# Where the 480-column tiles begin in SBUF: a fused attention and SwiGLU kernel

## The chip, the cores and the metric

The kernel runs on one core of one Trainium2 chip. The metric is the device time of one execution in microseconds; lower is better. Three runs of the kernel before gave 1454.55, 1455.09 and 1456.19 us, a median of 1455.09 us.

## The reference

Two stages, on 4 batches of 12416 rows of 128 float32 numbers. The first is an attention through 32 inducing rows, the second a SwiGLU with 1536 hidden columns:

```python
def mab(q, kv):
    s = scale * (q @ kv.transpose(0, 2, 1))
    s = s - s.max(-1, keepdims=True)
    a = np.exp(s)
    a /= a.sum(-1, keepdims=True) + 1e-09
    return a @ kv
h = mab(I, x)                 # 32 rows attend to the 12416 rows of a batch
x = mab(x, h)                 # each row attends to those 32 rows
...
g = x @ w_gate
silu = g * (1.0 / (1.0 + np.exp(-g)))
val = x @ w_val
return silu * val @ w_out
```

Some shortened; all of it is float32. The 49664 rows of the second stage are the output's rows.

## The kernel before, in words

Rows of a batch are handled as columns: a tile holds up to 512 rows of x side by side, and TensorE streams them past weights that are loaded first. A batch is cut into 25 column tiles (COLS): one of 512 columns, then four each for the six entries of FC that follow the first. FC = [4, 16, 16, 16, 15, 15, 15] counts blocks of 32, so that tiles 0 to 12 of a batch have 512 columns and tiles 13 to 24 have 480. Each tile goes through 12 steps t, one for each 128 of the 1536 hidden columns (NT).

The second attention is folded into the weights: for each batch its 32 averages are multiplied into w_gate and w_val, which gives tw (L392, two buffers of 3072 columns). What is left of x in a tile is a *stack*: 128 partitions with the attention's weights split into a high and a low part (a_hi, a_lo), copied together by four DMAs of SP's queue (spread, L490; L499). A stack lies in one of three slots.

For each tile and t there is a unit of work:
- front (L680): two matmuls, L691 and L692, with tw as the loaded weights and the stack as the stream. They give g and v in PSUM (tile gv).
- gate (L695): ACT takes silu of g (L697). value (L699): DVE multiplies by v (L705); the product h stays in PSUM for three of the twelve t.
- split (L707): ACT, in some units DVE, rounds h to h_hi (L713), and POOL, or DVE for three of the twelve t, takes the rest as h_lo (L715).
- back (L719): three matmuls into one PSUM bank o: h_hi past wo_lo (L729), h_hi past wo_hi (L730), h_lo past wo_hi (L731). After t = 11 DVE copies the bank out and SP stores it (L738, L740).

PE's order is fixed by the loop at L769: the front of one unit, then the back of a unit that is about five units older, then the next front. So L691, L692, L729, L730, L731 repeat, and before each matmul its weights are loaded (the PEld rows of a profile). Around a change of width the front is of one width and the back of the other for some five units. The next batch's attention is laid between the units by slots (plan, L561), nearly all of it in 512-column stretches of the batches before the last; batch 0 has its own start, written out as lists of tokens.

The stack, h_hi and h_lo are tiles of WB = WF + 64 = 576 columns (2304 bytes a partition), of which a tile of work uses up to 512. Where it begins in them is set by AT, in float32 elements, for the stack, h_hi and h_lo:

```python
AT = (16, 48, 48), (0, 0, 0)                                            # L37
return AT[u > NG * FC.count(max(FC))]                                   # L200, at(u): second triple from tile 13 on
st.stack[u] = stp.tile([P, WB], F32R, name="stack")[:, at(u)[0]:][:, :WF]   # L487
u.hi = hip.tile([P, WB], F32R, name="h_hi")[:, u.at[1]:u.at[1] + WF]        # L711
u.lo = lop.tile([P, WB], F32R, name="h_lo")[:, u.at[2]:u.at[2] + WF]        # L712
```

In the program's memory map, modulo 256 bytes in a partition, tw, wo_hi and wo_lo begin at 224, every slot of the stack at 160, every slot of h_hi and h_lo at 32. A piece of weights is 128 columns, 512 bytes, so every piece of them has the same remainder.

Of the kernel before, what the change touches and what calls it, by code (L numbers as in the profile page):

```python
# [33 lines left out]
W = 32 * max(CH)  # L34
WF = 32 * max(FC)
WB = WF + 64
AT = (16, 48, 48), (0, 0, 0)  # L37
NT = DFF // P
SCALE = 1.0 / math.sqrt(C)

# [65 lines left out]
def induced_set_attention_then_swiglu(ctx: ExitStack, tc: tile.TileContext, xt, xn, ind, wgv, wo, out):  # L106
# [91 lines left out]
    def at(u):  # L198

        return AT[u > NG * FC.count(max(FC))]  # L200

# [637 lines left out]
```

## Time and profile before

| | |
|---|---|
| median of three runs | 1455.09 us |
| span of the profiled execution | 1453.1 us |
| TensorE: share busy, granted clock | 99%, 1.000 |
| chain that ended last: share of TensorE | 95% |
| busy shares of ACT, POOL, DVE | 88%, 83%, 82% |
| front matmuls L691 over 512 / 480 columns | 624 / 576 |
| back matmuls L729 over 512 / 480 columns | 612 / 576 |

The span is the time from the first instruction to the last of the execution that was profiled; that execution has no separate time beside it, so the median of the runs stands for it, 2.0 us above the span. The chain of work is followed back from the last instruction to whatever released each step. Matmuls overlap each other, so that the length of one in the profile is longer than the distance between the starts of two.

### The profile page before, as it was taken

The numbers are of one execution on the slowest core, as the hardware profiler recorded it, in microseconds if no ns is written. First come the engines' busy times: TensorE is split into PE (matmuls) and PEld (weight loads), VectorE is DVE, ScalarE is ACT, GpSimd is POOL, SyncE is SP. The second block draws the span as 40 slices with busy tenths as digits, with TensorE's granted clock in tenths as the row PEclk, the third lists the DMA queues.
The fourth block names the chain that finished last, engine by engine and source line by source line (L and its number), as shares of the span: only waits on it lengthen the run. The fifth ranks groups of instructions, "written<-read, shape, count | busy, mean of one in ns | idle before, by whom it ended". The sixth has DMA issues, their size and how long they took to land.

```text
span 1453.1 us, 24926 instructions
## 1 busy us (share of the span) xinstructions
PE 1441.8 (99%) x7452; PEld 1173.5 (81%) x7452; DVE 1187.8 (82%) x2080; ACT 1281.9 (88%) x2388; POOL 1207.9 (83%) x995
## 2 busy tenths in 40 slices
PE   8999999999999999999999999999999999999999
PEld 5577788788887787888888778688888888888887
DVE  6888778887888788888788778988888878878877
ACT  5888898799998887999999888799999999999997
POOL 1689778888998778898899878879889889889987
PEclk9999999999999999999999999999999999999999
DMA  9233522321143242211123522321111111111110
GB/s 369 68 98 126 185 74 97 106 64 56 36 138 136 88 137 106 70 52 42 35 69 111 189 78 93 107 79 35 42 36 42 37 44 37 40 40 38 39 41 21
DMA packets 50822, 119.80 MB, mean 82 GB/s; under 512 B 11392, under 2 KB 28288, under 8 KB 50688
## 3 DMA queue, kind: packets, MB, share of 16 engines
q1 hardware_dynamic: 50688, 118.22, 24.9%
q8 instruction: 59, 0.97, 0.3%
q14 instruction: 75, 0.61, 0.1%
HBM read 62.87 MB, written 25.43 MB: 61 GB/s over the span
## 4 chain that ended last, share of the span: by engine, by line
PE 95%; DMA 2%; ACT 1%; POOL 1%; DVE 0%; SPq 0%; issue 0%; DVEq 0%; ACTq 0%; POOLq 0%
PE gv L691 18%; PE o L729 18%; PE gv L692 18%; PE o L730 18%; PE o L731 18%; PE gv L270 2%; PE o L318 1%; DMA s_all<-wgv 1%; DMA xt<-xt 1%; PE o L270 1%; PE o L727 1%; POOL h_lo L715 0%; ACT silu L697 0%; PE gv L420 0%; ACT h_hi L713 0%; PE gv L398 0%
## 5 line engine op out<-in xcount | busy, mean ns | idle before, releaser
L715 POOL TENSOR_TENSOR h_lo<-h,h_hi 128x512 fp32r<-128x512 f32 (+1 forms) x890 | 1110.9, 1273 | 198.4 <-ACT h_hi L713 140.4
L697 ACT ACTIVATE silu<-gv 128x512 f32<-128x512 f32 (+1 forms) x1200 | 704.7, 588 | 109.3 <-PE gv L691 76.3
L705 DVE TENSOR_TENSOR h<-gv,silu 128x512 f32<-128x512 f32 (+1 forms) x891 | 594.5, 668 | 199.0 <-ACT silu L697 147.7
L713 ACT CAST h_hi<-h 128x512 fp32r<-128x512 f32 (+1 forms) x788 | 474.7, 602 | 30.1 <-DVE h L705 25.3
L691 PE MATMUL gv<-stack,tw 128*128 128x512 f32 (+1 forms) x1200 | 465.9, 388 | 2.1 <-DVE stack L543 1.3
L692 PE MATMUL gv<-stack,tw 128*128 128x512 f32 (+1 forms) x1200 | 461.5, 385 | 0.7 <-ACT silu L697 0.4
L729 PE MATMUL o<-h_hi,wo_lo 128*128 128x512 f32 (+1 forms) x1188 | 458.4, 386 | 0.0
L730 PE MATMUL o<-h_hi,wo_hi 128*128 128x512 f32 (+1 forms) x1188 | 456.9, 385 | 0.0
L731 PE MATMUL o<-h_lo,wo_hi 128*128 128x512 f32 (+1 forms) x1188 | 456.3, 384 | 0.0
L691 PEld LDWEIGHTS gv<-stack,tw 128*128 128x128 f32 x1200 | 225.4, 188 | 50.5 <-ACT tw L412 2.6
L729 PEld LDWEIGHTS o<-h_hi,wo_lo 128*128 128x128 f32 x1188 | 223.0, 188 | 51.8 <-issue 12.1
L692 PEld LDWEIGHTS gv<-stack,tw 128*128 128x128 f32 x1200 | 224.9, 187 | 47.8 <-ACT silu L697 4.2
L731 PEld LDWEIGHTS o<-h_lo,wo_hi 128*128 128x128 f32 x1188 | 222.6, 187 | 40.5 <-POOL h_lo L715 0.4
L730 PEld LDWEIGHTS o<-h_hi,wo_hi 128*128 128x128 f32 x1188 | 223.1, 188 | 38.9
L705 DVE TENSOR_TENSOR gv<-gv,silu 128x512 f32<-128x512 f32 (+1 forms) x297 | 201.8, 680 | 40.2 <-ACT silu L697 39.1
L715 DVE TENSOR_TENSOR h_lo<-gv,h_hi 128x512 fp32r<-128x512 f32 (+1 forms) x297 | 197.3, 664 | 0.9
L713 ACT CAST h_hi<-gv 128x512 fp32r<-128x512 f32 (+1 forms) x294 | 167.5, 570 | 4.9 <-DVE gv L705 3.9
L738 DVE COPY ob<-o 128x512 f32<-128x512 f32 (+1 forms) x100 | 66.3, 663 | 0.8 <-PE o L731 0.8
L713 DVE CAST h_hi<-h 128x512 fp32r<-128x512 f32 (+1 forms) x103 | 52.0, 506 | 0.0
L483 POOL TENSOR_TENSOR a_lo<-aT,a_hi 128x480 fp32r<-128x480 f32 (+2 forms) x26 | 34.6, 1330 | 0.0
L190 POOL TENSOR_TENSOR wgv_sb<-s_all 128x512 int32<-128x512 int32 x2 | 2.9, 1455 | 28.9 <-ACT s_all L178 28.9
L467 POOL TENSOR_TENSOR s_all<-s_all,sm 128x512 f32<-128x512 f32 (+2 forms) x27 | 26.1, 967 | 0.0
(155 smaller groups left out, 476.2 us busy)
## 6 DMA issues: line engine op xcount, KB each, us to landing
xt_sb<-xt SPq DMA_DIRECT2D x32, 896.0 KB, 5.2
xn_sb<-xn SPq DMA_DIRECT2D x18, 896.0 KB, 5.6
out<-ob SPq DMA_DIRECT2D x52, 256.0 KB, 2.0
out<-ob SPq DMA_DIRECT2D x48, 240.0 KB, 2.0
stack<-a_hi SPq DMA_DIRECT2D x96, 64.0 KB, 2.0
stack<-a_lo SPq DMA_DIRECT2D x96, 64.0 KB, 2.0
stack<-a_hi SPq DMA_DIRECT2D x96, 60.0 KB, 2.0
stack<-a_lo SPq DMA_DIRECT2D x96, 60.0 KB, 2.0
```

The costliest lines, as they stand in the source:

```text
L270: nc.tensor.matmul(out=ps[32 * j:32 * j + 32, 32 * (lo - b0):32 * (hi - b0)], lhsT=lhsT, rhs=st.xt[q][:, lo - CH0[q]:hi - CH0[q], j, :], s ...
L483: eng.tensor_sub(out=st.al[q][:, :n], in0=st.at[q][:, :n], in1=st.ah[q][:, :n].bitcast(F32))
L691: nc.tensor.matmul(out=u.g[:, :n], lhsT=st.w[:, wcol(0, t)], rhs=rhs, start=True, stop=True)
L692: nc.tensor.matmul(out=u.v[:, :n], lhsT=st.w[:, wcol(1, t)], rhs=rhs, start=True, stop=True)
L697: nc.scalar.activation(out=u.s[:, :u.n], in_=u.g[:, :u.n], func=AF.Silu)
L705: nc.vector.tensor_mul(out=u.h[:, :n], in0=u.v[:, :n], in1=u.s[:, :n])
L713: (nc.vector.tensor_copy if u.cast_dve else nc.scalar.copy)(out=u.hi[:, :n], in_=u.h[:, :n])
L715: eng.tensor_sub(out=u.lo[:, :n], in0=u.h[:, :n], in1=u.hi[:, :n].bitcast(F32))
L729: nc.tensor.matmul(out=o[:, :n], lhsT=wo_lo[:, ws], rhs=u.hi[:, :n], start=(t == 0), stop=False)
L730: nc.tensor.matmul(out=o[:, :n], lhsT=wo_hi[:, ws], rhs=u.hi[:, :n], start=False, stop=False)
L731: nc.tensor.matmul(out=o[:, :n], lhsT=wo_hi[:, ws], rhs=u.lo[:, :n], start=False, stop=(t == NT - 1))
L738: nc.vector.tensor_copy(out=ob[:, :n], in_=o[:, :n])
```

## The change

One line: the second triple of AT. In tiles of 480 columns the stack begins 48 elements (192 bytes) into its slot, h_hi and h_lo 16 elements (64 bytes) into theirs, instead of at the start. Counted from the weights modulo 256 bytes, the stacks move from 192 to 128, both parts of h from 64 to 128. Tiles of 512 columns, at 0 from the weights, stay as they are; so do the slots' sizes, every instruction and its order.

```diff
-AT = (16, 48, 48), (0, 0, 0)
+AT = (16, 48, 48), (48, 16, 16)
```

## The prediction

> **What bounds the kernel now.** I read the page's busy shares first, then its chain of work that ended last, then the clock.
>
> ```profile
> PE 1441.8 (99%) x7452; PEld 1173.5 (81%) x7452; DVE 1187.8 (82%) x2080; ACT 1281.9 (88%) x2388; POOL 1207.9 (83%) x995
> PE 95%; DMA 2%; ACT 1%; POOL 1%; DVE 0%; SPq 0%; issue 0%; DVEq 0%; ACTq 0%; POOLq 0%
> core 0: 1453.1 us, clock 1.000
> ```
>
> TensorE is 95% of the chain at full granted clock, so the time is the sum of the intervals from one matmul's start to the next. A busy PE is not yet a PE at its peak, since matmuls overlap; only the starts tell what each costs. The next view, the instruction groups with shapes kept apart, says which matmuls the change reaches and that they wait for nobody ("idle before" is the last column).
>
> ```profile
> L691 PE MATMUL gv<-stack,tw 128*128 128x512 f32 x624 | 248.4, 398 | 2.1 <-DVE stack L543 1.3 <-DVE h L705 0.3 <-ACT tw L412 0.2
> ...
> L730 PE MATMUL o<-h_hi,wo_hi 128*128 128x480 f32 x576 | 218.4, 379 | 0.0
> L731 PE MATMUL o<-h_lo,wo_hi 128*128 128x480 f32 x576 | 217.8, 378 | 0.0
> L729 PE MATMUL o<-h_hi,wo_lo 128*128 128x480 f32 x576 | 217.6, 378 | 0.0
> L691 PE MATMUL gv<-stack,tw 128*128 128x480 f32 x576 | 217.5, 378 | 0.0
> L692 PE MATMUL gv<-stack,tw 128*128 128x480 f32 x576 | 217.2, 377 | 0.0
> ```
>
> There are 576 units of five matmuls (two of the front, three of the back) over 480 columns, 2880 matmuls, and 624 units that start over 512. Their 378 ns can't be the price, since neighbours overlap; I take starts from the timeline of PE instead. First a stretch of 512 columns alone, then one of 480 alone; each fence has a first row, a last row and one unit.
>
> ```profile
> 1149.83 0.39 PE L691 MATMUL gv<-stack,tw 128*128 128x512 f32 x1
> ...
> 1281.29 0.39 PE L691 MATMUL gv<-stack,tw 128*128 128x512 f32 x1
> ```
>
> ```profile
> 1319.77 0.38 PE L691 MATMUL gv<-stack,tw 128*128 128x480 f32 x1
> 1319.99 0.38 PE L692 MATMUL gv<-stack,tw 128*128 128x480 f32 x1
> 1320.20 0.38 PE L729 MATMUL o<-h_hi,wo_lo 128*128 128x480 f32 x1
> 1320.42 0.38 PE L730 MATMUL o<-h_hi,wo_hi 128*128 128x480 f32 x1
> 1320.63 0.38 PE L731 MATMUL o<-h_lo,wo_hi 128*128 128x480 f32 x1
> 1320.85 0.38 PE L691 MATMUL gv<-stack,tw 128*128 128x480 f32 x1
> ...
> 1438.57 0.38 PE L691 MATMUL gv<-stack,tw 128*128 128x480 f32 x1
> ```
>
> 131.46 us are 116 units of 512 columns: 1133.3 ns each, 226.7 per matmul. 118.80 us are 110 units of 480 columns: 1080.0 ns each, 216.0 per matmul. By columns alone the second should be 15/16 of the first, 1062.5. So a 480 unit pays 17.5 ns that a 512 unit does not. Both numbers are whole multiples of 13.33 ns, 85 and 81 of them; 15/16 of 85 is 79.7. I call 13.33 ns a step and come back to it.
>
> **The change part by part.** It adds and removes no instruction, wait or DMA. It moves where 480-column data begins inside slots that are 2304 bytes apart, nine times 256, so that a start has the same remainder modulo 256 in every slot. From the change's own statement (48 elements, 192 bytes, put the stack 128 bytes from the weights; 16 elements, 64 bytes, do so for h) the slots themselves begin at 192 bytes (stack) and 64 bytes (h_hi, h_lo) from the weights. Hence before: 480-column stacks begin at phase 192, both parts of h at 64. 512-column tiles, with 16 and 48 elements, all begin at phase 0. After: 480-column tiles all at phase 128.
>
> *The writers.* ACT, POOL and DVE write h_hi and h_lo, and SP's queue writes the stacks, at the new offsets. The before already has both cases, 512 columns at an offset and 480 at none:
>
> ```profile
> L715 POOL TENSOR_TENSOR h_lo<-h,h_hi 128x512 fp32r<-128x512 f32 x459 | 590.7, 1312 | 121.3 <-ACT h_hi L713 85.1 <-PE o L730 17.2 <-DVE h_hi L713 9.8
> L715 POOL TENSOR_TENSOR h_lo<-h,h_hi 128x480 fp32r<-128x480 f32 x431 | 520.5, 1233 | 77.1 <-ACT h_hi L713 55.3 <-DVE h_hi L713 13.9 <-PE o L731 3.9
> stack<-a_hi SPq DMA_DIRECT2D x96, 64.0 KB, 2.0
> stack<-a_hi SPq DMA_DIRECT2D x96, 60.0 KB, 2.0
> ```
>
> 1233/1312 is 0.940 beside 480/512 = 0.938, and both DMA rows land in 2.0 us: the offset costs writers nothing. If it cost them a little, two things would cover it: PE's zero idle in the 480 rows above, and these busy shares in a stretch of 480 columns alone:
>
> ```profile
> core 0: us, PE busy (x) PEld busy (x) DVE busy (x) ACT busy (x) POOL busy (x), PEclk, DMA share, GB/s
> 1320.00:1440.00 120.00, 120.00 (x557) 104.18 (x556) 95.82 (x164) 111.40 (x214) 103.99 (x87) 1.00 0.12 35
> ```
>
> 120 us are 111.1 units, so ACT works 1003 ns and POOL 936 ns in each of 1080. Should PE get faster, ACT is next, at 1003 ns. With the cover gone a slower writer would show as PE waiting for L713 or L715. I take 0.
>
> *The readers.* This is the term that counts. While a matmul streams stack or h, the weights of the next are loaded:
>
> ```profile
> 700.11 0.38 PE L691 MATMUL gv<-stack,tw 128*128 128x480 f32 x1
> 700.33 0.38 PE L692 MATMUL gv<-stack,tw 128*128 128x480 f32 x1
> ```
>
> ```profile
> 700.11 0.19 PEld L692 LDWEIGHTS gv<-stack,tw 128*128 128x128 f32 x1
> 700.33 0.19 PEld L729 LDWEIGHTS o<-h_hi,wo_lo 128*128 128x128 f32 x1
> ```
>
> A load takes 0.19 us of an interval of 0.216, and starts at the start of a matmul, so both streams leave their starting addresses together: a fixed phase between them can matter in every one of the 2880 matmuls. The trace of before has no 480-column tile at phase 128, so its price has to be bounded. The mixed stretches, where front and back have different widths, give the other end:
>
> ```profile
> 407.65 0.39 PE L691 MATMUL gv<-stack,tw 128*128 128x512 f32 x1
> ...
> 408.77 0.39 PE L691 MATMUL gv<-stack,tw 128*128 128x512 f32 x1
> ...
> 409.89 0.39 PE L691 MATMUL gv<-stack,tw 128*128 128x512 f32 x1
> ```
>
> ```profile
> 1292.61 0.38 PE L691 MATMUL gv<-stack,tw 128*128 128x480 f32 x1
> ...
> 1294.88 0.38 PE L691 MATMUL gv<-stack,tw 128*128 128x480 f32 x1
> ```
>
> Front 512 and back 480: 1120 ns, 84 steps. Front 480 and back 512: 2.27 us in two units, 1135 ns, 85.1 steps. Count 17 steps for a 512 matmul (85/5) and 16 for a 480 one (79.7/5, rounded), and these should be 2 x 17 + 3 x 16 = 82 and 2 x 16 + 3 x 17 = 83. So a unit pays over the count: 0 steps where all five starts have one phase (512 alone), 1 with phases 192 and 64 (480 alone), 2 with 0 and 64, 2 with 192 and 0.
>
> Best end: after, all five starts have one phase again, the extra is 0 and a unit takes 80 steps, 1066.7 ns, 13.3 ns less; over 576 units 7.7 us. Scaled without rounding it is 17.5 ns, 10.1 us. Worst end: an extra of 2, as in the mixed units: 13.3 ns more, 7.7 us. I take the best end, since the row nearest to the new state is that of 512 columns alone, the only one with a single starting phase. Another reason points the same way. 480 columns are 1920 bytes, 128 more than a multiple of 256, so a stream begun at 128 ends at 0; a 512 stream begun at 0 ends at 0 too. Seen from its end the new layout is the one that the 512 tiles have.
>
> The skill speaks against any effect. The Trainium skill, TensorE: Matmul & The Clock Gate, in Step-by-step: what each phase is for, says that TensorE has two independent read ports and that loading the next weights takes no bandwidth from the running matmul; phases would then be worth nothing and the time would stay. The trace sides with it only in part, as 216.0 against 212.5 ns (226.7 x 15/16) is left unexplained. The same page, Back-to-back issue gap, gives N/2.4 + 2.5 ns, 202.5 for 480 columns; the trace has 216.0, and if the change reached that rule the gain would be an estimated 39 us.
>
> The 35 or so units in mixed stretches change their phases also; 35 units by one step are 0.5 us either way, inside the range.
>
> The sum is 1453.1 - 7.7 = 1445.4 us of span. The median of the runs is 1455.1, 2.0 us above this profiled span, and the three runs lie from 1454.6 to 1456.2; I put the 2.0 us on top as the same before and after: 1447.4 us.
>
> **The rivals.**
>
> *A, one phase is as good as for 512 columns: 80 steps, 1447.4 us.* For it: the four kinds of stretch above. Against it: only one of them has a single phase. Chance 0.45. A deeper gain belongs beside it, 79 steps or fewer, 1439.7 us or less, bounded by ACT's 1003 ns at 44 us; nothing in the trace shows a matmul below 16 steps, so 0.05.
>
> *B, the phase isn't what costs the step: 81 steps stay, 1455.1 us.* The step would then belong to 480 columns as such, and moving the starts does nothing. This is what the rule of two ports amounts to. For it: in one 480 unit, starts at phase 192 and at 64 cost alike, 0.22 and 0.21 us for the two front rows, 0.22, 0.21 and 0.22 for the back rows above, though their phases differ by 128. Against it: the mixed units pay a step more with the same widths. Chance 0.20.
>
> *C, the jump between streams costs: slower.* A stream ends at its start plus 128 (480 columns) or at its start (512), and the next begins elsewhere. In 512 alone no hand-over jumps: 0 extra steps. In 480 alone three of five do (stack to stack, h_hi to h_hi, h_hi to h_lo), and front to back and back to front do not, since the stack ends at 64, where h begins: 1 extra. In the mixed units four and three jump: 2 extra each. By these three, 5 steps in 10 jumps, a jump costs half a step. After the change all five hand-overs jump by 128: an extra of 2 to 2.5 instead of 1. At 2 a unit takes 82 steps, 13.3 ns more, 1462.8 us; at 2.5 1466.6. It decides as soon as five jumps cost more than the three of today. For it: the count fits as well as A's. Against it: in the unit shown the two hand-overs without a jump aren't visibly shorter (0.21 and 0.22 us). Chance 0.30.
>
> **How the numbers follow.** Differences under 0.2%, 2.9 us, are about what runs that spread over 1.6 us can't tell from no change. A and its deeper form are faster, 0.50; B the same, 0.20; C slower, 0.30. The range has to reach over both signs: from 1444, which takes in A with the unrounded 10.1 us and the mixed units, to 1464, which takes in C at two steps. Outside are the deeper gain and C at 2.5 steps, under 0.2 together. A's own range is 1444 to 1449.
>
> **What would show it.** In the timeline of the changed kernel a unit in a 480 stretch takes 1066.7 ns (A), 1080.0 (B) or 1093.3 (C), with that of 512 columns still 1133.3; the time moves by 576 times the difference. PE's idle before L691 to L731 stays near zero, else a writer has become late. POOL's L715 over 480 columns stays at 1233 ns and the stack's DMAs at 2.0 us. I am wrong if one phase doesn't mean one price: if the starting distance of 128 bytes is a bad one where 0 is a good one, or if the ends and starts have to meet.

## The result and the profile after

The change made the kernel slower: 1464.67 us, median of five runs (1464.07 to 1465.18), beside 1454.58 us, also of five runs, for the kernel before; the ratio is 1.0066, 95% interval 1.0054 to 1.0079. I had forecast 1447.4 us with a range up to 1464.0. The page after has the same engine in the same place, with more time in it:

```profile
span 1462.7 us, 24926 instructions
PE 1453.5 (99%) x7452; PEld 1174.1 (80%) x7452; DVE 1198.9 (82%) x2080; ACT 1278.5 (87%) x2388; POOL 1201.4 (82%) x995
PE 98%; ACT 1%; DVE 1%; POOL 0%; issue 0%; DMA 0%; POOLq 0%; DVEq 0%; ACTq 0%
```

The number of instructions is that of before, ACT and POOL worked slightly less, and DVE 11.1 us more. The groups of instructions and the DMA issues show that no writer became late (idle before PE's rows is 0.0):

```profile
L729 PE MATMUL o<-h_hi,wo_lo 128*128 128x480 f32 x576 | 219.6, 381 | 0.0
L691 PE MATMUL gv<-stack,tw 128*128 128x480 f32 x576 | 219.3, 381 | 0.0
...
L715 POOL TENSOR_TENSOR h_lo<-h,h_hi 128x480 fp32r<-128x480 f32 x431 | 518.7, 1226 | 91.0 <-ACT h_hi L713 62.0 <-PE o L730 14.6 <-DVE h_hi L713 10.3
...
L713 DVE CAST h_hi<-h 128x512 fp32r<-128x512 f32 (+1 forms) x103 | 63.6, 618 | 0.0
...
stack<-a_hi SPq DMA_DIRECT2D x96, 60.0 KB, 1.9
```

One writer does work longer. DVE's casts to h_hi took 52.0 us before and take 63.6 us now; the 49 of them over 480 columns rose from 437 to 676 ns each. The address of h_hi isn't the reason: in e3 below h lies where it lies before, and these casts take 659 ns. What lengthens them stays open, and PE doesn't wait for them. So the time lies between the starts of matmuls. The timeline of PE, first and last start of a long stretch, 480 columns and then 512:

```profile
1340.21 0.38 PE L691 MATMUL gv<-stack,tw 128*128 128x480 f32 x1
...
1449.11 0.38 PE L691 MATMUL gv<-stack,tw 128*128 128x480 f32 x1
```

```profile
1150.95 0.39 PE L691 MATMUL gv<-stack,tw 128*128 128x512 f32 x1
...
1281.28 0.39 PE L691 MATMUL gv<-stack,tw 128*128 128x512 f32 x1
```

108.90 us are 99 units of 1100.0 ns, against 1080.0 before: 82.5 steps of 13.33 ns instead of 81. 130.33 us are 115 units of 512 columns, 1133.3 ns as before. In batch 0 the same change gave two prices in one stretch. A unit took 1100 ns up to 295 us, where other matmuls come between two units (5.5 us more than a unit), and after them this:

```profile
306.63 0.38 PE L691 MATMUL gv<-stack,tw 128*128 128x480 f32 x1
...
391.56 0.38 PE L691 MATMUL gv<-stack,tw 128*128 128x480 f32 x1
```

84.93 us are 78 units of 1088.8 ns. The sum holds: 416 pure units of the later batches at 20.0 ns more are 8.3 us, 130 of batch 0 at 11.0 more 1.4 us, the mixed units together 0.1 us less, 9.6 us in all; the spans differ by 1462.7 - 1453.1 = 9.6 us.

### The profile page after: what moved, and what is told of

It is laid out like the page before. It is cut to its first block, busy times and chain, and to the rows that moved or that the text cites. A ratio compares the mean times of both kernels' runs of the same rounds, so it can differ in the third digit from the quotient of the medians.

```text
span 1462.7 us, 24926 instructions
## 1 busy us (share of the span) xinstructions
PE 1453.5 (99%) x7452; PEld 1174.1 (80%) x7452; DVE 1198.9 (82%) x2080; ACT 1278.5 (87%) x2388; POOL 1201.4 (82%) x995
## 4 chain that ended last, share of the span: by engine, by line
PE 98%; ACT 1%; DVE 1%; POOL 0%; issue 0%; DMA 0%; POOLq 0%; DVEq 0%; ACTq 0%
PE o L729 18%; PE gv L692 18%; PE gv L691 18%; PE o L730 18%; PE o L731 18%; PE gv L270 2%; PE o L318 1%; PE o L270 1%; PE o L727 1%; PE gv L262 0%; PE gv L642 0%; PE gv L420 0%; ACT silu L697 0%; PE gv L398 0%; PE o L371 0%; POOL h_lo L715 0%
## 5 line engine op out<-in xcount | busy, mean ns | idle before, releaser
L691 PE MATMUL gv<-stack,tw 128*128 128x512 f32 (+1 forms) x1200 | 467.7, 390 | 1.6 <-DVE stack L543 0.8
L692 PE MATMUL gv<-stack,tw 128*128 128x512 f32 (+1 forms) x1200 | 463.6, 386 | 0.7 <-ACT silu L697 0.4
L729 PE MATMUL o<-h_hi,wo_lo 128*128 128x512 f32 (+1 forms) x1188 | 460.6, 388 | 0.0
L730 PE MATMUL o<-h_hi,wo_hi 128*128 128x512 f32 (+1 forms) x1188 | 458.0, 386 | 0.0
L731 PE MATMUL o<-h_lo,wo_hi 128*128 128x512 f32 (+1 forms) x1188 | 457.6, 385 | 0.0
L691 PEld LDWEIGHTS gv<-stack,tw 128*128 128x128 f32 x1200 | 224.9, 187 | 51.5 <-ACT tw L412 2.6
L729 PEld LDWEIGHTS o<-h_hi,wo_lo 128*128 128x128 f32 x1188 | 222.7, 187 | 53.8 <-issue 12.1
L692 PEld LDWEIGHTS gv<-stack,tw 128*128 128x128 f32 x1200 | 224.9, 187 | 49.2 <-ACT silu L697 4.0
L731 PEld LDWEIGHTS o<-h_lo,wo_hi 128*128 128x128 f32 x1188 | 222.7, 187 | 43.4 <-POOL h_lo L715 0.4
L730 PEld LDWEIGHTS o<-h_hi,wo_hi 128*128 128x128 f32 x1188 | 222.7, 187 | 41.8
L713 DVE CAST h_hi<-h 128x512 fp32r<-128x512 f32 (+1 forms) x103 | 63.6, 618 | 0.0
```

Of the source, the lines that this page charges most:

```text
L691: nc.tensor.matmul(out=u.g[:, :n], lhsT=st.w[:, wcol(0, t)], rhs=rhs, start=True, stop=True)
L692: nc.tensor.matmul(out=u.v[:, :n], lhsT=st.w[:, wcol(1, t)], rhs=rhs, start=True, stop=True)
L713: (nc.vector.tensor_copy if u.cast_dve else nc.scalar.copy)(out=u.hi[:, :n], in_=u.h[:, :n])
L729: nc.tensor.matmul(out=o[:, :n], lhsT=wo_lo[:, ws], rhs=u.hi[:, :n], start=(t == 0), stop=False)
L730: nc.tensor.matmul(out=o[:, :n], lhsT=wo_hi[:, ws], rhs=u.hi[:, :n], start=False, stop=False)
L731: nc.tensor.matmul(out=o[:, :n], lhsT=wo_hi[:, ws], rhs=u.lo[:, :n], start=False, stop=(t == NT - 1))
```

## The experiments

After the result two theories were left. J, the prediction's rival C: a hand-over between streams that jumps costs half a step. P: a matmul's price depends on the phase of its stream to the weights. All runs below change the kernel *before*, which had medians of 1454.85 to 1455.34 us beside them. "A unit" is the mean distance between starts of the first front matmul in a pure stretch. A time without a ratio is that of a single run; there the distances in the trace carry the argument.

### Other common phases for 480 columns

```diff
-AT = (16, 48, 48), (0, 0, 0)
+AT = (16, 48, 48), (16, 48, 48)   # e1, phase 0
+AT = (16, 48, 48), (0, 32, 32)    # e2, phase 192
+AT = (16, 48, 48), (32, 0, 0)     # e3, phase 64
```

> 480-column stacks and both parts of h at phase 0 from the weights, as the 512-column tiles have; nothing else changed. Theory J (a hand-over whose next stream does not begin where the last one ended costs half a step of 13.33 ns): any common phase gives five jumps of 128 bytes a unit, so 1100.0 ns a unit and 1464.7 us, as at phase 128. Theory P (a matmul's price is set by its phase to the weights; 0 is the good one and 128 the bad one): 1066.7 ns a unit, 1447 us.

> 480-column stacks and both parts of h all at phase 192. J: 1100.0 ns a unit, as for every common phase. P: the unit of before has phases 192 and 64 and takes 1080.0; at 192 alone it takes something between 1066.7 and 1093.3, not 1100.

> 480-column stacks and both parts of h all at phase 64. J: 1100.0 ns a unit. P: between 1066.7 and 1093.3, and with the run at 192 averaging about 1080 (two front matmuls at 192 and three back ones at 64 make 1080.0).

Phase 0 (e1): 1456.09 us, ratio 1.0008 (0.9999 to 1.0018), no difference clear of the noise. Phase 192 (e2): 1454.82 us. Phase 64 (e3): 1461.13 us. The timeline of e1, then of e2:

```profile
1310.85 0.38 PE L691 MATMUL gv<-stack,tw 128*128 128x480 f32 x1
...
1428.94 0.37 PE L691 MATMUL gv<-stack,tw 128*128 128x480 f32 x1
```

```profile
1311.08 0.38 PE L691 MATMUL gv<-stack,tw 128*128 128x480 f32 x1
...
1429.88 0.38 PE L691 MATMUL gv<-stack,tw 128*128 128x480 f32 x1
```

109 units of 1083.4 ns and 110 of 1080.0; e3 has 1091.7. All of them have the five jumps of 128 bytes that the change has, and none costs 1100. J falls. P's number for phase 0, 1066.7, is missed as well: one phase, even the phase of the 512-column tiles, isn't enough.

### Phase 128 for 512 columns

```diff
-AT = (16, 48, 48), (0, 0, 0)
+AT = (48, 16, 16), (0, 0, 0)
```

> 512-column tiles at phase 128 instead of 0, 480-column tiles as in the kernel before. J: a 512-column stream ends where the next begins at any common phase, so 1133.3 ns a unit of 512 columns stay and the time is that of before within 3 us. P: if 128 costs a 480-column matmul 220.0 - 213.3 = 6.7 ns more than 0, it does so here: 1166.7 ns a unit, 33.3 ns more in some 620 units, 20 us slower.

```profile
1150.32 0.39 PE L691 MATMUL gv<-stack,tw 128*128 128x512 f32 x1
...
1289.14 0.40 PE L691 MATMUL gv<-stack,tw 128*128 128x512 f32 x1
```

138.82 us are 119 units of 1166.6 ns, as P said, though not one hand-over jumps at this width. The time is 1468.88 us, 14 more rather than 20: in the three stretches with attention's work between the units, the mean unit rose by 11 to 23 ns and not by 33.

### What the phase is measured from

e5 puts an unused tile of 128 bytes ahead of everything. e9 puts one ahead of the weights and another behind them, so that weights move and streams stay (modulo 256):

```diff
+    moved = const.tile([P, 32], F32, name="moved")      # e5: before ident; e9: before wgv_sb
+    nc.gpsimd.memset(moved, 0.0)
...
-    pad = sgl.tile([P, 32], F32, name="pad")
+    pad = sgl.tile([P, 64], F32, name="pad")            # e9 alone
```

> The kernel before with an unused 128-byte tile ahead of all others, so that weights, stacks and both parts of h all move by 128 bytes and their phases to each other stay. Theory R (what counts is the phase between streams and weights): 1133.3 ns a unit of 512 columns and 1080.0 of 480 stay, 1454.8 us. Theory A (what counts is each stream's own address modulo 256): the 512-column tiles then behave as they did when they alone moved by 128 bytes, 1166.7 ns a unit, and the time is 10 us or more above that of before.

> The kernel before with tw, wo_hi and wo_lo 128 bytes further on, by an unused 128-byte tile ahead of them and another behind them; stacks, h and all tiles of the units' other engines keep their remainders modulo 256. Theory R (the reference of the phases is the weights): 512-column tiles are then at phase 128 and take 1166.7 ns a unit, as when they were moved themselves; about 14 us slower. Rival (the reference is something else that TensorE's streams share with the other engines, such as where ACT and POOL write): nothing changes, 1133.3 and 1080.0.

e5 took 1454.79 us, with units of 1133.3 and 1080.0 ns: moving everything together by 128 bytes changes nothing, so the address by itself doesn't count. e9 took 1475.31 us. Its timeline, 512 columns and then 480 (L693 is L691 there):

```profile
1150.96 0.39 PE L693 MATMUL gv<-stack,tw 128*128 128x512 f32 x1
...
1299.68 0.40 PE L693 MATMUL gv<-stack,tw 128*128 128x512 f32 x1
```

```profile
1331.04 0.38 PE L693 MATMUL gv<-stack,tw 128*128 128x480 f32 x1
...
1449.12 0.38 PE L693 MATMUL gv<-stack,tw 128*128 128x480 f32 x1
```

128 units of 1161.9 ns, near e4's 1166.6 (both runs show both prices, in different stretches), and 108 of 1093.3, where the sweep below has 1093.2 for the same phases (stack 64, h 192) reached by moving the streams. The reference of the phases is the weights.

### The load beside the stream

```diff
-    nc.tensor.matmul(out=o[:, :n], lhsT=wo_hi[:, ws], rhs=u.hi[:, :n], ...)
+    nc.tensor.matmul(out=o[:32, :n], lhsT=wo_hi[:, P * t:P * t + 32], rhs=u.hi[:, :n], ...)   # e11: 64 for 32; L731 likewise
```

> The kernel before with L730 and L731 loading 32 of the 128 weight columns and writing 32 of the 128 output rows (the other 96 rows lack these two products). Same streams, same phases. Theory L (what a matmul pays over its columns comes from the load that runs beside it): L729 runs beside L730's load and L730 beside L731's, now a quarter as long, so these two intervals fall, by three quarters of 13.3 ns if the 17th step of a 512-column matmul is the load's: from 226.7 to about 217 ns, a unit from 1133.3 to about 1113, while L691, L692 and L731, which run beside whole loads, keep 226.7. Rival (the extra belongs to the stream, or to the hand-over from stream to stream): all intervals stay, 1133.3 and 1080.0.

> As the run with loads of 32 columns, with 64 columns in L730 and L731 (the last 64 of the 128 output rows lack these two products). A load of 32 columns walks 128 bytes, one of 64 columns 256. Theory W with the loads' walk counted as well (a load that ends half a period off is a jump too): 64 columns end where they began, so a 512-column unit is back at 1133.3 ns or below, and 480 at about 1080. Rival (loads of changing width cost in themselves): it stays clearly above 1133.3, between that and the 1160 of the run with 32.

The load of L730 falls to 0.11 us in e6, but the units grow:

```profile
1150.78 0.11 PEld L730 LDWEIGHTS o<-h_hi,wo_hi 128*32 128x32 f32 x1
```

```profile
1150.31 0.39 PE L691 MATMUL gv<-stack,tw 128*128 128x512 f32 x1
...
1289.51 0.39 PE L691 MATMUL gv<-stack,tw 128*128 128x512 f32 x1
```

139.20 us are 120 units of 1160.0 ns, against 1133.3; with 64 columns a unit takes 1146.7 (480 columns: 1091.1 and 1079.9). In e6 all five distances of a 512-column unit grew from 226.7 ns: that of L729, beside L730's shorter load, to 229.1, that of L730, beside L731's, to 233.0, the others to between 231.0 and 234.7. The whole times are 1471.85 and 1460.22 us. Both theories of the load miss: a shorter load is not cheaper, and 64 columns, a full walk of 256 bytes, don't bring 1133.3 back. The rival on record for e11, that loads of changing width cost in themselves, fits its 1146.7 but not its 480 columns, which stay at 1079.9. The two matmuls also write only 32 or 64 of the 128 output rows here, which these runs don't separate from the load.

### The two parts of the change

```diff
-AT = (16, 48, 48), (0, 0, 0)
+AT = (16, 48, 48), (48, 0, 0)     # e7, stacks alone
+AT = (16, 48, 48), (0, 16, 16)    # e8, both parts of h alone
```

> The stack's part of the change alone: 480-column stacks at phase 128, h at 64. If each matmul pays by its own phase (common phases measured 1083.3 ns a unit at 0, 1091.7 at 64, 1100.0 at 128, 1080.0 at 192), two matmuls at 128 and three at 64 give 1095.0 ns, 8.6 us above before. If prices do not add up but depend on the order of the phases, it is another number; before, with 192 and 64, is already such a case, 1080.0 where adding gives 1087.

> The other part alone: 480-column stacks stay at phase 192, both parts of h at 128. If prices add: two matmuls at 192 and three at 128 give 1092.0 ns a unit, 6.9 us above before. If both this and the stack's part alone cost less than half of the change's 9.8 us, the loss needs the common phase of 128.

1458.68 and 1459.60 us, units of 1086.7 and 1088.9 ns. Prices do not add: 1095.0 and 1092.0 were the sums. The two parts cost 3.8 and 4.7 us, together 8.5 of the change's 10; in units they add 6.7 and 8.9 of its 20.0 ns. So neither alone is the culprit.

### Many phases in one run

Since a unit's price can be read from a few units, one run can hold many layouts: AT is looked up by batch and tile, so that each 480-column tile, and each 512-column tile, has its own phases (e10, e12 and g2).

```diff
-        return AT[u > NG * FC.count(max(FC))]
+        s, hi, lo = PHASES[12 * b + (u - 1) % 12] if u else (0, 0, 0)
+        return ((s - 192) % 256 // 4, (hi - 64) % 256 // 4, (lo - 64) % 256 // 4)
```

> Each of the 48 tiles of 480 columns, and of the 48 of 512 (the first tile of a batch aside), gets another combination of phases for the stack, h_hi and h_lo, in steps of 64 bytes; the price of a combination is read from the units in which front and back are of one tile. If a common phase of 0 is best for 512 columns because nothing jumps, no other of the 48 comes under 1133.3 ns. If one phase for all three were the point, combinations with one phase would be the cheapest for 480 columns; so far 0, 64, 128 and 192 gave 1083.3, 1091.7, 1100.0 and 1080.0, and 192 with 64 gave 1080.0, so I expect none under 1066.7 and the cheapest near 1080.

> The sweep with other phases: 12 common ones in steps of 16 bytes that are no multiples of 64, combinations of 32, 96, 160 and 224, and eight with h_lo 192 bytes behind h_hi. If 1080.0 ns is the least that 480 columns can have (27 combinations of 64-byte steps came to it or within 7 ns, none below), none comes below here. If the grid of 64 bytes was the limit, some phase off it comes to 1066.7, which would be worth 7.7 us.

> The sweep with common phases in steps of 4 bytes, those that are no multiples of 16. If the price follows lines of 16 bytes, phases off them cost as much as a neighbour on them or more, and none is under 1066.7 ns (480 columns) or 1133.3 (512). If single bytes count, there may be cheaper ones for either width.

In steps of 64 bytes (e10) the least for 480 columns is 1080.0 ns, reached by twelve combinations, only one of them (192) a common phase; for 512 columns, where attention's work left the units readable, all but phase 0 have 1146 or more on average. The change's own layout reads about 1088 there, the lower of its two prices, so a price from a few units need not be that of a long stretch. In steps of 16 bytes (e12) my expectation was missed: the common phases 112 and 144, 16 bytes on either side of the change's 128, take 1066.7. In steps of 4 bytes (g2) neighbours differ by more than the whole change. Timeline of g2, phases 168, 172 and 180 for 480 columns, then 196 for 512; four units each (L692 is L691 there):

```profile
1067.80 0.38 PE L692 MATMUL gv<-stack,tw 128*128 128x480 f32 x1
...
1072.20 0.38 PE L692 MATMUL gv<-stack,tw 128*128 128x480 f32 x1
...
1080.83 0.37 PE L692 MATMUL gv<-stack,tw 128*128 128x480 f32 x1
...
1085.09 0.37 PE L692 MATMUL gv<-stack,tw 128*128 128x480 f32 x1
...
1093.78 0.38 PE L692 MATMUL gv<-stack,tw 128*128 128x480 f32 x1
...
1098.25 0.38 PE L692 MATMUL gv<-stack,tw 128*128 128x480 f32 x1
```

```profile
1146.97 0.40 PE L692 MATMUL gv<-stack,tw 128*128 128x512 f32 x1
...
1151.77 0.40 PE L692 MATMUL gv<-stack,tw 128*128 128x512 f32 x1
```

That is 1100, 1065 (1066.7 by the finer times of the trace), 1117 and, for 512 columns, 1200 ns a unit. The dearest 480-column phase, 100, has 1133.3. Sixteen of the 47 phases that could be read have 1066.7, one of them, 12, in two units alone, and none less; for 512 columns phase 252 has 1133.3, again none less. Both floors are columns/32 plus one step per matmul: 16 and 17 steps.

The phases of g2 also fall into groups by their remainder modulo 16 bytes. With remainder 4, all 15 that could be read for 480 columns end at 1098.7 ns or more (the mean of a tile's last three units); with remainder 12, twelve of 16 end at 1066.7 and the other four at 1077.7 to 1092.0. For 512 columns remainder 4 gives 1164 to 1200, remainder 12 1133 to 1165. Remainder 8 has both (1066.7 to 1100 for 480 columns), and so have the multiples of 16 in e12, so this is no full rule. The sweep also takes the remainders in the same order throughout, so it doesn't separate the effect of a tile's phase from that of the tile ahead of it.

### Other widths

```diff
-FC = [4, 16, 16, 16, 15, 15, 15]
+FC = [4, 16, 16, 16, 16, 16, 13]    # f1: 416 columns, second triple (0, 0, 0)
+FC = [4, 16, 16, 16, 16, 15, 14]    # e13: 480 as before, 448 at phase 0
...
+        return AT[FC[COLS[u][0]] == 15]   # e13 alone
```

> The last six entries of FC are 16, 16, 16, 16, 16, 13 instead of 16, 16, 16, 15, 15, 15: the same columns in five entries of 512-column tiles at phase 0 and one of 416 columns (second triple 0, 0, 0). If 512 columns at phase 0 are the cheap form at 17 steps and what a narrower tile pays over its columns is about the same per matmul as for 480 (16.2 steps for 15/16 of the columns), 576 units at 1080.0 ns become 384 at 1133.3 and 192 at about 947: 622 us become 617, 5 us faster. If 416 columns are as dear as the change's 480 (16.5 steps, 1.5 over the columns), 192 units at 967 make it 1 us faster.

> The last six entries of FC are 16, 16, 16, 16, 15, 14: one of 480 columns at phases 192 and 64 as before, and one of 448 at phase 0. 448 columns are 1792 bytes, seven times 256, so that a stream ends at the phase where the next begins, as with 512. Theory W (a matmul costs one step over its columns where all phases are 0 and no hand-over jumps; 480 columns cannot have that, for they end 128 bytes off): 448 columns take 14 + 1 steps each, 1000.0 ns a unit. Rival (only 512 is cheap; narrower tiles pay 1.2 steps whatever the phase, as 480 and 416 at their best): 1013.3 ns a unit.

f1 took 1450.62 us, ratio 0.9968 (0.9956 to 0.9979): 946.7 ns a unit of 416 columns, and the gain of 4.4 us is near the 5 that I worked out. In e13 (1452.46 us) a unit of 448 columns takes this:

```profile
1402.47 0.36 PE L691 MATMUL gv<-stack,tw 128*128 128x448 f32 x1
...
1443.00 0.36 PE L691 MATMUL gv<-stack,tw 128*128 128x448 f32 x1
```

40 units of 1013.3 ns, not 1000.0: 448 columns end where the next stream begins and still pay 1.2 steps a matmul, where 480 columns at phase 112, with five jumps, pay 1. The jump doesn't set the price.

### A version that beats both

```diff
-AT = (16, 48, 48), (0, 0, 0)
+AT = (16, 48, 48), (44, 12, 12)
```

> 480-column stacks and both parts of h at the common phase 112, 16 bytes short of the change's 128. The sweep had 1066.7 ns a unit there in the last units of one tile, 213.3 per matmul. If that is a state that lasts over whole stretches, 576 units at 13.3 ns less than before make 7.7 us: 1447.3 us, 0.9947 of before. If it was a stretch of transition after the neighbouring tile, units go back to 1080 or more and the time is that of before or above.

1446.63 us, ratio 0.9945 (0.9932 to 0.9958). Its timeline and windows:

```profile
1300.24 0.38 PE L691 MATMUL gv<-stack,tw 128*128 128x480 f32 x1
...
1429.31 0.38 PE L691 MATMUL gv<-stack,tw 128*128 128x480 f32 x1
```

```profile
1310.00:1430.00 120.00, 120.00 (x565) 105.17 (x564) 97.19 (x166) 111.98 (x216) 105.53 (x89) 1.00 0.12 36
```

129.07 us are 121 units of 1066.7 ns, and it lasts over whole stretches in all four batches. The windows' row has ACT busy 111.98 of 120 us, so ACT isn't in the way. The mixed units fall to 1093.3 and 1106.7, 82 and 83 steps, exactly the count that the prediction called the price without extra; with these 23 and 27 ns less the gain reaches 8.4 us where 7.7 was expected. This is the gain forecast for the change, 16 bytes away from it.

## Why the prediction was wrong

- **The writers at 0: right for the time, not for every writer.** POOL's rows have 1226 ns where they had 1233, the stack's DMAs 1.9 us, and PE waits for no one. But DVE's 49 casts over 480 columns, for which the prediction showed no row, take 676 ns where they took 437; the cover that it named, PE's zero idle, held.
- **The term that counts, its 576 units and its place: right.** The units' distances give all of the 9.6 us.
- **The step that failed: "I take the best end, since the row nearest to the new state is that of 512 columns alone, the only one with a single starting phase."** A single phase does not make a unit cheap: 0, 64, 128 and 192 gave 1083.4, 1091.7, 1100.0 and 1080.0 ns (e1 to e3 and the change). I inferred a cause from four stretches that differed in width and in phases at once. In place of the 13.3 ns less that I took, a unit at 128 cost 20.0 ns more.
- **The second reason, the stream seen from its end: wrong.** Streams of 480 columns at 112 end at 240 and cost 1066.7; 448 columns at 0 end at 0 and pay 1.2 steps.
- **The worst end, 2 extra steps: too small.** It came from the mixed units, which bound nothing; one of the two rows was also misread, as 1135 ns were two units of a stretch whose five average 1129.6, 1.7 extra steps and not 2. The change has 2.5 extra steps, and phase 100 has 5. My range ended 0.7 us below the result.
- **Rival A** did not come, and its deeper form of 79 steps appears in none of the phases tried. **Rival B** fell with the result: the step is no property of 480 columns (80 steps at 112).
- **Rival C hit the time, 1462.8 to 1466.6, by its half step per jump: five of them are 2.5, which is 82.5 steps.** Its mechanism is refuted: the same five jumps go with 1066.7 to 1133.3 ns, and 512 columns at 128 pay 1166.6 without one. A right number is no proof of a cause.
- **The Trainium skill, TensorE: Matmul & The Clock Gate, Step-by-step: what each phase is for**, has two independent read ports and a load that takes nothing from the running matmul. The prediction drew from it that phases would be worth nothing; that these runs contradict, as moving the weights alone by 128 bytes cost 20 us (e9). Whether it is read bandwidth that a bad phase costs, no run shows. The formula of the Trainium skill, same page, Back-to-back issue gap, is given there for a single matmul; the spacing estimated from it, 202.5 ns for 480 columns and 215.8 for 512, was not reached at any phase tried. The least mean distances in units with whole loads were 213.3 and 226.7.

What stays open: by which rule a phase gets its price. Shown are its reference (the weights), a grain no coarser than 4 bytes (the least step tried), a floor of one step that no phase undercut, that prices of parts don't add, and that one layout can hold two lasting prices (1088.8 and 1100 in one stretch). That load and stream conflict in some part of the partition's memory would fit, but a shorter load did not help, so this is argued and not shown.

## What to carry to other kernels

Where one engine's matmuls follow each other without idle time, read the distance between their starts by shape, and look for shapes that don't cost in proportion to columns. If the stream's starting offset to the weights matters, don't reason from another width: give each tile of one run another offset, in single elements, and read the prices from its units. Confirm the best one over whole stretches, since neighbours 4 bytes apart differed by up to 50 ns a unit (1133.3 at phase 100, 1083 at 104), and a price can change after an interruption.

## What I had not expected of the hardware

Steps of 4 bytes in the distance between streams and weights move a 480-column unit between 1066.7 and 1133.3 ns and a 512-column unit between 1133.3 and 1200.0, at full granted clock and without idle time of PE in these stretches. The settled distances repeat for a hundred units and are often whole multiples of 13.33 ns per unit or per few units. Loading 32 instead of 128 weight columns in two of five matmuls made the 512-column unit dearer, 1160.0 against 1133.3 ns.
